# A linear-attention and MLP block on one core: the attention matrix is split one pair of chunks later, the first residual rows are asked for later, and two blocks of the matrix are copied with their column sets apart

## The chip, the cores and the metric

The kernel runs on one core of one Trainium2 chip. The metric is the device time of one launch in microseconds (us). Before the change it is 403.99 us, the median of 3 runs (402.62 to 404.39). TensorE is called PE, its weight loads PEld; VectorE is DVE, ScalarE is ACT, GpSimd is POOL and SyncE is SP. Each engine works through its own instructions in order; ACT, DVE and PE read and write on-chip tiles, SP and POOL issue the transfers (DMAs) used here, and POOL also does a little arithmetic.

## The reference

x is normalised over its 512 features, and the normalised xn goes into two branches that are added to x. All is float32.

```python
B, S, D, F, H = 1, 2048, 512, 1376, 32
xn = (x - mean(x)) / sqrt(var(x) + 1e-5)
# attention, heads of 16 features
q, k, v = split(xn @ wqkv)
phi = lambda t: where(t > 0, t + 1, exp(t)) + 1e-6
kv  = einsum("bhsd,bhse->bhde", phi(k), v)
z   = einsum("bhsd->bhd", phi(k))
o   = einsum("bhqd,bhde->bhqe", phi(q), kv) / (einsum("bhqd,bhd->bhq", phi(q), z) + 1e-6)
A   = o.reshape(B, S, D) @ wo
# MLP
h   = relu(xn @ w1 + b1) ** 2
out = x + A + (h @ w2 + b2)
```

## The kernel before

Each float32 operand of a large product is held as two parts, a high one (name ending in h, or index 0) and a low one (l, or index 1), whose sum is the number. ACT writes the high part as a copy with rounding, DVE subtracts it from the source to give the low part, and PE adds three products (high by high, high by low, low by high) in one PSUM bank. The helper `split` does the two steps; the copy is recorded at line 121 and the subtraction at line 129 or 132.

The program has four stages. First x is normalised, turned and multiplied by the key weights, and the 512 by 512 sums over tokens are gathered (lines 384 and 404). From them comes the attention matrix: kv of each head times its rows of wo, 512 by 512, in four row chunks j = 0 to 3 (`matrix`, `matrix_copy`). `matrix_copy` leaves chunk j in a raw tile `m`, two chunks to a tile, in the pool places x0 and x1; `matrix_parts(j)` then splits chunk j into `mh` and `ml` (the tiles `m[0]` and `m[1]`, 128 by 4 by 512: partition, chunk, output column).

The **first pair** are the last two blocks of 512 tokens (t1 = 3, t2 = 2). A loop `for p in range(NO + 1)` with NO = 7 goes over pairs of 128-wide chunks of the query and MLP weights (order q, w, q, w, w, w, w), two chunks by two blocks of tokens at a time. It uses seven products in place of eight (Strassen and Winograd), so each pair needs sums of weight blocks (`aop`, split into high and low) and sums of token blocks (`T[1]` to `T[4]`). In each p the four banks b0 to b3 take the products; ACT copies one (`c12`) out of its bank before PE adds to that bank again. In between `mlp_2` multiplies the squared activations of an earlier chunk by its rows of w2 into the banks `acc`. A table AT sets how many steps of the attention division (phi, weighted sum, quotient, split) go into each gap. After the loop `add_attention` multiplies the attention rows by `mh` and `ml` into `acc` for t1, and DVE adds each `acc` to the residual rows `res` (line 1096), which are then stored. `load_res(t)` asks SP for the four residual tiles of a block as two transfers of 512 KB into x0 and x1; `add_bias` has POOL add b2 onto them by four accumulating transfers of 256 KB (line 1088). Then the MLP of t2 goes on: nine `mlp_2`, numbered e = 0 to 8 below, of twelve matmuls each, their w2 parts made by ACT and DVE just ahead; attention of t2; and the last two chunks (`sum_2`). The `w2t` tiles hold sums of w2 blocks that are made there for the second pair (`w2_sums`, loads at line 1113, subtractions at 1118, stores to `w2sd` at 1121); they lie in the places B0, B1 and A0, from which the first pair's T tiles have gone and into which the second pair's T tiles are to come.

The **second pair** (t1 = 1, t2 = 0) does the chunk pairs again with operands that were stored, and then also the second product by the seven-product scheme, over output columns LO (0 to 255) and HI (256 to 511) and over pairs of rows. `mul` (line 1694) does one of the seven, M1 to M7; its part "q" is the attention's share, with the attention matrix as the stationary operand (PE loads 128 by 128 of it, then streams 512 tokens). There an output block of 256 columns is wanted as its even and its odd columns, e = 0 and 1. For operands that are sums (`mt`) they lie apart already; for the three plain blocks of `m` the helper `columns` picks every second column as PE loads the weights. M1 uses rows 0 and 1, columns LO (b11); M2 uses rows 2 and 3, columns LO (b21); M3 uses rows 2 and 3, columns HI (b22) as the moving operand, without `columns`.

Of the kernel before, what the change touches and what calls it, by code (L numbers as in the profile page):

```python
# [13 lines left out]
P = 128  # L14
# [4 lines left out]
def kernel(  # L19
# [30 lines left out]
    nc = tc.nc  # L50
# [30 lines left out]
    def bank(name, tag="ps"):  # L81
        return psum.tile([P, 512], F32, name=name, tag=tag)
# [11 lines left out]
    def two(name):  # L94
        return work.tile([P, 2, 512], F32, name=name, tag=next_tag("x"))
# [7 lines left out]
    def four(name, tag, dt=F32, pool=None):  # L103
        return (pool or work).tile([P, TB, 512], dt, name=name, tag=tag)
# [5 lines left out]
    def f32(ap):  # L110
        return ap.bitcast(F32)
# [7 lines left out]
    def copy(eng, o, i, bias=0.0):  # L119
        if eng == "act":  # L120
            nc.scalar.activation(o, i, AF.Copy, bias=bias)  # L121
        elif bias:
            ENG[eng].tensor_scalar(o, i, bias, None, op0=OP.add)
        else:
            ENG[eng].tensor_copy(o, i)
# [18 lines left out]
    def both(name, tags, dt=F32R, pool=keep):  # L144
        return [pool.tile([P, NJ, D], dt, name=f"{name}{u}", tag=t) for u, t in zip("hl", tags)]
# [262 lines left out]
    q = {}  # L408
# [151 lines left out]
    t, rk = two("x0"), four("rk", "r0")  # L560
# [7 lines left out]
    t = two("x2")  # L568
# [17 lines left out]
    for i0 in range(0, NT, TB):  # L586
        a = first_xp[i0]
# [5 lines left out]
        if i0 < NPE:  # L593
            single = work.tile([P, 3, 512], F32, name=f"xg{i0}s", tag="r0")
            for k in range(3):
                i = i0 + k - 1
# [3 lines left out]
        for k in range(0, n, 2):  # L600
            i = i0 + TB - n + k
            u, v = (t.rearrange("p a (g c) -> p (a g c)", g=NJ) for t in (a[:, TB - n + k:][:, :2], o[:, k:k + 2]))
            groups[i + 1] = [t.rearrange("p (g n) -> p g n", g=NJ) for t in (u, v)]
            u, v = (t.rearrange("p (g i c) -> p g i c", g=NJ, i=2) for t in (u, v))
# [24 lines left out]
    for k in range(2):  # L629
        a = slice(k * D // 2, (k + 1) * D // 2)  # L630
# [125 lines left out]
    def load_1(kind, n):  # L756
        load = raw_1 if kind == "w" else raw_q
        return [load(2 * n + k).rearrange("p (c n) -> p c n", c=2) for k in range(2)]
# [69 lines left out]
    def columns_low(x, t):  # L828

        for a in range(0, NJ, 2):  # L830
            rest_of(x[1][:, a:a + 2], t[:, a:a + 2], x[0][:, a:a + 2])
# [13 lines left out]
    for i in range(2, NT):  # L845
# [13 lines left out]
        ps = pks[i] if i < 3 else bank(f"pk{i}")  # L859
# [28 lines left out]
        if i == 12:  # L888
            w = load_1("q", 0)
# [67 lines left out]
    m = both("m", ("mh", "ml"), pool=work)  # L957
# [37 lines left out]
    def matrix_parts(j):  # L995
        split(m[0][:, j, :], m[1][:, j, :], mraw[j // 2][:, j % 2], "act", "dve")
# [6 lines left out]
    LO, HI = slice(0, D // 2), slice(D // 2, D)  # L1003
# [34 lines left out]
    NO = len(order)  # L1038
# [12 lines left out]
    def load_operand(p, name):  # L1051

        if p >= NO:
            return
        s, c = OPERANDS[name]
        if p % 2 == 0 and name != "A22":
            o = raw_at(f"{name}_{p}", (P, 2, 256), F32R)
        else:
            k = 7 if p % 2 == 0 else ALL_OPS.index(name)
            o = slots[k // 4][:, k % 4]  # L1060
        nc.sync.dma_start(f32(o), aopd[p][s][:, :, c * 256 % aopd[p][s].shape[-1]:][:, :, :256])
        held_ops[p][name] = [o[:, u] for u in range(2)]
# [6 lines left out]
    def second_loads():  # L1069
        slots.update({k: keep.tile([P, 4, 2, 256], F32R, name=f"slot{k}", tag=f"xT{NB // 2 + k}") for k in range(2)})  # L1070
        load_operand(0, "A22")
        for name in ALL_OPS:
            load_operand(1, name)

    def load_res(t):
        for k in range(2):
            r = two(f"res{t}_{k}")
            i = t * TB + 2 * k
            nc.sync.dma_start(r, xf[i * P:(i + 2) * P, :].rearrange("(i p) d -> p i d", i=2))
            for i in range(2):  # L1080
                res[t, 2 * k + i] = r[:, i, :]
            biased.append(r)
# [27 lines left out]
    def w2_sums(k, n, tag):  # L1110

        t = keep.tile([P, 2, 2, 512], F32, name=f"w2t{k}", tag=tag)[:, :n]
        nc.sync.dma_start(t.rearrange("p k c d -> p (k c) d"),
                          w2[2 * k * P:2 * (k + n) * P, :].rearrange("(a p) d -> p a d", p=P))
        (b11, b12), (b21, b22) = ([t[:, :, c, a] for a in (slice(0, D // 2), slice(D // 2, D))] for c in range(2))

        def less(o, x, y):
            return lambda: nc.vector.tensor_tensor(out=o, in0=x, in1=y, op=OP.subtract)

        return [less(b11, b12, b11), less(b12, b22, b12), less(b22, b22, b11), less(b21, b21, b22),  # L1120
                lambda: nc.sync.dma_start(w2sd[:, k:k + n], t)]
# [46 lines left out]
    w = load_1(*order[1])  # L1168
# [20 lines left out]
    for p in range(NO + 1):  # L1189
        at_p = AT[p]  # L1190
        kind, k = order[p] if p < NO else ("", 0)
# [64 lines left out]
        if p == 1:  # L1256
            nc.vector.tensor_scalar(zc[:, 1], zc[:, 0], 1e-6, 1e-6 * H / D, op0=OP.mult, op1=OP.add)
            acc = [bank(f"acc{t1}_{k}", "acc") for k in range(TB)]
        for j in {3: (0,), 4: (1,), 5: (2, 3)}.get(p, ()):
            matrix_parts(j)  # L1260
        step(at_p[8])
        if was == "w":
# [18 lines left out]
        if p + 2 < NO:  # L1281
            w = load_1(*order[p + 2])
# [48 lines left out]
        if p == NO - 1:  # L1331
            for k, (count, tag) in enumerate(((2, "B0"), (2, "B1"), (1, "A0"))):
                w2_prepare += w2_sums(2 * k, count, tag)
        if p == NO - 2:
            load_res(t1)
        if p == NO - 1:
            bias = add_bias()

    def wait_for(f):
# [94 lines left out]
    for k in range(TB):  # L1434
        add_attention(acc, t2 * TB + k)
        if k == 0:
# [2 lines left out]
                wait_for(f)  # L1439
            columns_low(x1, f1)  # L1440
    second_loads()
    for k in range(TB):
        for j, f in enumerate(last_two):
            sum_2(acc[k], k, f, j == 1)
        add(acc[k], t2, k)
        store(t2, k)
# [149 lines left out]
    def left_now(name, *which):  # L1596
        for part in which:
# [3 lines left out]
    RIGHT = {"M4": ("T4", "t", 1, LO), "M1": ("b11", "m", 0, LO), "M2": ("b21", "m", 1, LO), "M6": ("T2", "t", 1, HI),  # L1601
             "M5": ("T1", "t", 0, LO), "M7": ("T3", "t", 0, HI), "M3": ("b22", "m", 1, HI)}
# [72 lines left out]
    def rights(name, part):  # L1675

        key, kind, r, at = RIGHT[name]
        if part == "q":
            return [[(m if kind == "m" else mt)[u][:, 2 * r + i, at] for u in range(2)] for i in range(2)]
        return [part_at[key, k] for k in ((0, 1), (2, 3), (4,))[part]]  # L1680

    def columns(w, e, half=0):
        return w[..., half * 256:(half + 1) * 256].rearrange("p (c e) -> p e c", e=2)[:, e]

    def mul(name, ps, *which, first=False):

        for part in which:
            chunks = list(zip(half_units[name, part], rights(name, part)))
            order = [(c, e, *uv) for c in range(len(chunks)) for e in range(2) for uv in PASSES]
            order.sort(key=(lambda o: o[1]) if part == "q" else (lambda o: o[3]))  # L1690
            for c, e, u, v in order:
                a, b = chunks[c]
                w = columns(b[u], e) if part == "q" and RIGHT[name][1] == "m" else b[u][:, e * P:(e + 1) * P]
                nc.tensor.matmul(ps[e], lhsT=w, rhs=a[v], start=first and c == u == v == 0, stop=False,  # L1694
                                 skip_group_check=True)
            first = False

# [138 lines left out]
    for p in range(NO):  # L1836
        kind, k = order[p]
# [72 lines left out]
    mt = w2_start["mt"]  # L1910
# [63 lines left out]
    for parts in ((0, 1), (2, "q")):  # L1974
        chunks = [(a, b) for part in parts for a, b in zip(half_units["M3", part], rights("M3", part))]
        for k in range(TB):
            for n, (a, b) in enumerate(chunks):
                three(ends[k], [v[:, k * P:(k + 1) * P] for v in a], b, False, "q" in parts and n == len(chunks) - 1)
            if "q" in parts:
                nc.vector.tensor_tensor(out=rows[:, k], in0=ends[k], in1=rows[:, k], op=OP.add)  # L1980
                i = t1 * TB + k
# [29 lines left out]
```

## Time and profile before

| | value |
|---|---|
| median of 3 runs | 403.99 us (402.62 to 404.39) |
| the profiled execution | 403.1 us |
| its span, first to last instruction | 401.0 us |
| granted PE clock in it | 0.998 |
| DVE busy | 318.2 us, 537 instructions |
| ACT busy | 259.6 us, 434 instructions |
| POOL busy | 63.1 us, 102 instructions |
| mean DMA rate | 218 GB/s |

A row of the timeline gives the start in us from the span's start, the time taken, the engine, the line, the operation, out<-in with shapes and a count; in brackets stands the idle time before it and what ended that. Several matmuls or copies are pipelined: a matmul's row shows 0.39 us, and twelve in a row take 2.72 us, so one comes every 0.227 us. A row of the windows gives a stretch and then, for each engine, its busy time and count, the granted clock, the share of the DMA engines' time and GB/s.

### The profile page before, as it was taken

How to read it: one execution, taken by the hardware profiler on the slowest of the kernel's cores; microseconds unless marked ns; L12 is line 12 of the kernel's file. 1: busy time of each engine (PE TensorE's matmuls, PEld its weight loads, DVE VectorE, ACT ScalarE, POOL GpSimd, SP SyncE). 2: the span in 40 equal slices, each digit the busy share in tenths (PEclk: the TensorE clock that was granted, in tenths of full speed). 3: DMA queues.
4: the chain of work that ended last, by engine and by line, in shares of the span. 5: the costliest groups of instructions: out<-in, count | busy, mean ns of one | idle time of the engine just before them, and what ended most of it. 6: DMA issues, size and time to landing. Idle time of an engine off the chain costs nothing.

```text
span 401.0 us, 5834 instructions
## 1 busy us (share of the span) xinstructions
PE 394.7 (98%) x1940; PEld 326.3 (81%) x1940; DVE 318.2 (79%) x537; ACT 259.6 (65%) x434; POOL 63.1 (16%) x102
## 2 busy tenths in 40 slices
PE   7999999999999999999999999999999999999996
PEld 6788888888788877888878888888888888888895
DVE  5886666498799988997599997439999896898771
ACT  5677777556887689889555863366688666475510
POOL 5444333220410000020000200010000000232300
PEclk9999999999999999999999999999999999999999
DMA  6857647821698747689696893897798698799983
GB/s 215 274 163 240 212 157 210 230 56 30 218 329 298 259 132 254 233 269 319 213 414 266 197 209 101 286 260 236 232 270 257 188 311 178 142 226 186 172 184 108
DMA packets 80093, 87.56 MB, mean 218 GB/s; under 512 B 26304, under 2 KB 61248, under 8 KB 79296
## 3 DMA queue, kind: packets, MB, share of 16 engines
q1 hardware_dynamic: 76160, 78.27, 62.7%
q0 software_dynamic: 3824, 8.92, 12.3%
q8 instruction: 15, 0.25, 0.3%
q14 instruction: 14, 0.11, 0.1%
q10 hardware_dynamic: 80, 0.00, 0.0%
HBM read 52.05 MB, written 28.84 MB: 202 GB/s over the span
## 4 chain that ended last, share of the span: by engine, by line
PE 94%; DMA 2%; DVE 1%; ACT 1%; issue 0%; SPq 0%; ACTq 0%
PE b L528 20%; PE acc L140 18%; PE pk L384 11%; PE kx L404 11%; PE a L1694 7%; PE b_c L528 5%; PE b_a L528 4%; PE end L140 2%; PE b L1694 2%; PE y L1694 2%; PE d L1694 2%; PE b_b L528 2%; PE pz L140 1%; DMA rk<-in_A_wqkv_dram 1%; PE acc L539 1%; DMA r<-in_B_w_dram 1%
## 5 line engine op out<-in xcount | busy, mean ns | idle before, releaser
L140 PE MATMUL acc<-w2r,s 128*128 128x512 f32 x240 | 57.0, 390 | 0.0
L140 PEld LDWEIGHTS acc<-w2r,s 128*128 128x128 f32 x240 | 44.9, 188 | 9.9 <-issue 0.4
L404 PE MATMUL kx<-pk,tok 128*128 128x512 f32 x192 | 46.0, 389 | 0.0
L528 PE MATMUL b<-T,aop 128*128 128x512 f32 x168 | 42.0, 391 | 0.2 <-ACT c L121 0.2
L404 PEld LDWEIGHTS kx<-pk,tok 128*128 128x128 f32 x192 | 36.0, 188 | 7.6 <-ACT pk L121 0.2
L528 PEld LDWEIGHTS b<-T,aop 128*128 128x128 f32 x168 | 31.3, 188 | 8.1 <-ACT t L121 0.8
L365 POOL TENSOR_TENSOR tok<-xp,tok 128x512 fp32r<-128x512 f32 x15 | 19.8, 1321 | 40.0 <-ACT tok L121 40.0
L1088 POOL DMA_DIRECT2D res<-in_B_b_dram x8 | 7.1, 1012 | 108.5 <-DVE S L766 60.1
L132 DVE TENSOR_TENSOR M<-h,M 128x1024 fp32r<-128x1024 f32 (+1 forms) x15 | 15.2, 1037 | 5.0 <-ACT M L121 5.0
L121 ACT ACTIVATE T<-Tf 128x512 fp32r<-128x512 f32 x16 | 9.4, 623 | 15.0 <-DVE Tf L709 14.9
L1629 POOL DMA_DIRECT2D h<-h x6 | 5.3, 926 | 85.1 <-issue 64.5
L528 PE MATMUL b<-xs0h,aop 128*128 128x512 f32 x56 | 18.5, 392 | 0.0
L121 ACT ACTIVATE M<-h 128x1024 fp32r<-128x1024 f32 (+1 forms) x15 | 13.2, 908 | 7.5 <-PE a L1694 2.8
L121 ACT ACTIVATE pk<-k 128x512 fp32r<-128x512 f32 x16 | 10.1, 630 | 8.7 <-DVE k L379 8.7
L140 PE MATMUL acc<-mh,aTsr 128*128 128x512 f32 x48 | 15.6, 390 | 0.0
L375 ACT ACTIVATE k<-pk 128x512 f32<-128x512 f32 x16 | 9.5, 593 | 8.6 <-PE pk L384 8.6
L392 DVE SCALAR_TENSOR_TENSOR pk<-k,pk 128x512 fp32r<-128x512 f32 x16 | 11.3, 709 | 4.5 <-ACT pk L121 3.4
L132 DVE TENSOR_TENSOR w2r<-r,w2r 128x512 fp32r<-128x512 f32 (+2 forms) x20 | 13.6, 682 | 0.5 <-ACT w2r L121 0.4
L242 DVE BATCH_NORM_STATS2 st<-x 128x6 f32<-128x512 f32 x16 | 10.9, 684 | 3.6 <-DMA x<-in_A_x_dram 3.5
L384 PE MATMUL pk<-wkh,xs1h 128*128 128x512 f32 x32 | 12.7, 396 | 0.4 <-ACT xs1h L332 0.4
L379 DVE SCALAR_TENSOR_TENSOR k<-pk,k 128x512 f32<-128x512 f32 x16 | 10.8, 675 | 2.6 <-ACT k L377 2.5
L121 ACT ACTIVATE w2r<-r 128x512 fp32r<-128x512 f32 x18 | 11.1, 620 | 2.6 <-DMA r<-in_B_w_dram 2.6
(398 smaller groups left out, 1062.6 us busy)
## 6 DMA issues: line engine op xcount, KB each, us to landing
r<-in_B_w_dram SPq DMA_DIRECT2D x26, 256.0 KB, 4.8
aop_0d<-aop SPq DMA_DIRECT2D x7, 512.0 KB, 4.3
aop_1d<-aop SPq DMA_DIRECT2D x7, 512.0 KB, 5.4
aop_2d<-aop SPq DMA_DIRECT2D x7, 512.0 KB, 5.9
via<-xp SPq DMA_DIRECT2D x5, 512.0 KB, 2.6
xg<-via SPq DMA_DIRECT2D x20, 128.0 KB, 2.8
xTd<-t SPq DMA_DIRECT2D x8, 256.0 KB, 4.3
x<-in_A_x_dram SPq DMA_DIRECT2D x4, 512.0 KB, 4.1
```

The costliest lines, as they stand in the source:

```text
L121: nc.scalar.activation(o, i, AF.Copy, bias=bias)
L132: nc.vector.tensor_tensor(out=l, in0=src, in1=f32(h), op=OP.subtract)
L140: nc.tensor.matmul(ps, lhsT=a[u], rhs=b[v], start=first and n == 0, stop=last and n == 2)
L242: nc.vector.bn_stats(st[:, k, :], xr[tiles[k]])
L365: ENG[el].tensor_tensor(out=l, in0=src, in1=f32(h), op=OP.subtract)
L375: nc.scalar.activation(p, ps, AF.Relu, scale=-1.0)
L379: nc.vector.scalar_tensor_tensor(p, ps, 0.0, p, op0=OP.max, op1=OP.add)
L384: nc.tensor.matmul(ps, lhsT=cols(i)[u][:, j, slot(i)], rhs=w[v][:, j, :], start=first and n == 0, stop=last and n == len(steps) - 1)
L392: nc.vector.scalar_tensor_tensor(pk[i][:, 1], p, 1e-6, f32(pk[i][:, 0]), op0=OP.add, op1=OP.subtract)
L404: nc.tensor.matmul(kxp[c], lhsT=tok[i][:, u, c * P:(c + 1) * P], rhs=pk[i][:, v], start=i == 0 and (u, v) == first, stop=i == NT - 1 and ( ...
L528: nc.tensor.matmul(ps, lhsT=a[u][:, j * P:(j + 1) * P], rhs=b[v][:, j, :], start=first and j == 0 and n == 0, stop=last and j == 1 and n == 2,
L1694: nc.tensor.matmul(ps[e], lhsT=w, rhs=a[v], start=first and c == u == v == 0, stop=False, skip_group_check=True)
```

## The change

It has three parts.

1. `matrix_parts` for chunks 0, 1 and 2 with 3 is called at p = 4, 5 and 6 in place of 3, 4 and 5.
2. `load_res(t1)` is called at p = 6, behind the loads of `w2_sums`, in place of p = 5. (It takes the tiles out of which `matrix_parts` reads.)
3. After the last `add_attention` of the first pair, which is the last to read b12 and the old place of b11, ACT copies b11 of `mh` and `ml` to rows 0 and 1, columns HI, and then b21 to rows 0 and 1, columns LO, each with its even and odd columns apart. `mul` then reads b11 and b21 there as plain 128-column blocks.

```diff
--- before.py
+++ after.py
@@ -1256,7 +1256,7 @@
         if p == 1:
             nc.vector.tensor_scalar(zc[:, 1], zc[:, 0], 1e-6, 1e-6 * H / D, op0=OP.mult, op1=OP.add)
             acc = [bank(f"acc{t1}_{k}", "acc") for k in range(TB)]
-        for j in {3: (0,), 4: (1,), 5: (2, 3)}.get(p, ()):
+        for j in {4: (0,), 5: (1,), 6: (2, 3)}.get(p, ()):
             matrix_parts(j)
         step(at_p[8])
         if was == "w":
@@ -1331,9 +1331,8 @@
         if p == NO - 1:
             for k, (count, tag) in enumerate(((2, "B0"), (2, "B1"), (1, "A0"))):
                 w2_prepare += w2_sums(2 * k, count, tag)
-        if p == NO - 2:
+        if p == NO - 1:
             load_res(t1)
-        if p == NO - 1:
             bias = add_bias()
 
     def wait_for(f):
@@ -1439,6 +1438,10 @@
                 wait_for(f)
             columns_low(x1, f1)
     second_loads()
+    for r, to in ((0, HI), (1, LO)):
+        for t in m:
+            copy("act", t[:, :2, to].rearrange("p i (e c) -> p i e c", e=2),
+                 f32(t[:, 2 * r:2 * r + 2, LO]).rearrange("p i (c e) -> p i e c", e=2))
     for k in range(TB):
         for j, f in enumerate(last_two):
             sum_2(acc[k], k, f, j == 1)
@@ -1676,7 +1679,10 @@
 
         key, kind, r, at = RIGHT[name]
         if part == "q":
-            return [[(m if kind == "m" else mt)[u][:, 2 * r + i, at] for u in range(2)] for i in range(2)]
+            t = m if kind == "m" else mt
+            if key in ("b11", "b21"):
+                r, at = 0, HI if key == "b11" else LO
+            return [[t[u][:, 2 * r + i, at] for u in range(2)] for i in range(2)]
         return [part_at[key, k] for k in ((0, 1), (2, 3), (4,))[part]]
 
     def columns(w, e, half=0):
@@ -1690,8 +1696,7 @@
             order.sort(key=(lambda o: o[1]) if part == "q" else (lambda o: o[3]))
             for c, e, u, v in order:
                 a, b = chunks[c]
-                w = columns(b[u], e) if part == "q" and RIGHT[name][1] == "m" else b[u][:, e * P:(e + 1) * P]
-                nc.tensor.matmul(ps[e], lhsT=w, rhs=a[v], start=first and c == u == v == 0, stop=False,
+                nc.tensor.matmul(ps[e], lhsT=b[u][:, e * P:(e + 1) * P], rhs=a[v], start=first and c == u == v == 0, stop=False,
                                  skip_group_check=True)
             first = False
```

On ACT, in the pair p = 3, the rows before are these. `mh<-m` is the high part of chunk 0, `aTsr<-q` an attention split, `aop<-r` the next operands, `c_3_1645<-b` is c12, which frees the bank.

```order
L423 ACTIVATE phi<-b_0_1214 128x512
L424 ACTIVATE phi<-phi 128x512
L121 ACTIVATE mh<-m_1276 128x512
L490 ACTIVATE c_3_1566<-c_3_1566 128x512
L121 ACTIVATE s_2_1622<-c_3_1566 128x512
L121 ACTIVATE aop_0_1125<-r_4_1515 128x512
L121 ACTIVATE aTsr_1208<-q_1206 128x512
L121 ACTIVATE c_3_1645<-b_1_1215 128x512
L121 ACTIVATE aop_1_1126<-r_5_1517 128x256
```

Now the row `mh<-m` is gone from there, and c12 stands one row earlier.

```order
L423 ACTIVATE phi<-b_0_1214 128x512
L424 ACTIVATE phi<-phi 128x512
L490 ACTIVATE c_3_1566<-c_3_1566 128x512
L121 ACTIVATE s_2_1620<-c_3_1566 128x512
L121 ACTIVATE aop_0_1125<-r_4_1515 128x512
L121 ACTIVATE aTsr_1208<-q_1206 128x512
L121 ACTIVATE c_3_1643<-b_1_1215 128x512
L121 ACTIVATE aop_1_1126<-r_5_1517 128x256
```

On SP, at the end of the first pair's loop, the two residual loads (`res`) stood ahead of the last stores of operands and the loads of `w2t`.

```order
L1079 DMA res_0_1939<-in_A_x_dram 128x2x512
L1079 DMA res_1_1941<-in_A_x_dram 128x2x512
L1046 DMA aop_0d<-aop_0_1125 128x1024
L1046 DMA aop_3d<-aop_1_1126 256x1x256
L1046 DMA aop_1d<-aop_0_1125 128x1024
L173 DMA r_9_1972<-in_B_w_dram 128x512
L1046 DMA aop_2d<-aop_1_1126 128x1024
L1113 DMA w2t_2063<-in_B_w_dram 128x4x512
L1113 DMA w2t_2065<-in_B_w_dram 128x4x512
L1113 DMA w2t_2067<-in_B_w_dram 128x2x512
L1365 DMA xT_2105<-xTd_93 128x2048
L1366 DMA xT_2106<-xTd_92 128x2048
```

They now stand behind the third `w2t` load and ahead of the two `xT` loads and the five loads of w2 rows (`r`).

```order
L1046 DMA aop_0d<-aop_0_1125 128x1024
L1046 DMA aop_3d<-aop_1_1126 256x1x256
L1046 DMA aop_1d<-aop_0_1125 128x1024
L173 DMA r_9_1964<-in_B_w_dram 128x512
L1046 DMA aop_2d<-aop_1_1126 128x1024
L1113 DMA w2t_2059<-in_B_w_dram 128x4x512
L1113 DMA w2t_2061<-in_B_w_dram 128x4x512
L1113 DMA w2t_2063<-in_B_w_dram 128x2x512
L1079 DMA res_0_2065<-in_A_x_dram 128x2x512
L1079 DMA res_1_2067<-in_A_x_dram 128x2x512
L1364 DMA xT_2105<-xTd_93 128x2048
L1365 DMA xT_2106<-xTd_92 128x2048
```

On ACT, between the first and the second pair, `s_2_0` is the last activation split of the first pair, `T` are high parts for the second pair, `d<-b_a` is the second pair's first copy out of a bank.

```order
L121 ACTIVATE s_2_10_2487<-r2c 128x512
L490 ACTIVATE r2c<-r2c 128x512
L121 ACTIVATE s_2_0_2492<-r2c 128x512
L121 ACTIVATE T_1018<-Tf_2109 128x512 x2
L121 ACTIVATE T_1_2239<-Tf_2109 128x512 x2
L121 ACTIVATE d_2615<-b_a 128x512
```

The four copies of the attention matrix now stand ahead of the last four T rows; each has 128 partitions by 512 elements.

```order
L121 ACTIVATE s_2_10_2487<-r2c 128x512
L490 ACTIVATE r2c<-r2c 128x512
L121 ACTIVATE s_2_0_2492<-r2c 128x512
L121 ACTIVATE mh<-mh 128x2x256
L121 ACTIVATE ml<-ml 128x2x256
L121 ACTIVATE mh<-mh 128x2x256
L121 ACTIVATE ml<-ml 128x2x256
L121 ACTIVATE T_1018<-Tf_2109 128x512 x2
L121 ACTIVATE T_1_2239<-Tf_2109 128x512 x2
L121 ACTIVATE d_2619<-b_a 128x512
```

## Prediction

> **What bounds the kernel now.** I read the page first, then PE's waits, then the two places where the change takes work off PE's path, and last the transfers that it moves.
>
> ```profile
> PE 394.7 (98%) x1940; PEld 326.3 (81%) x1940; DVE 318.2 (79%) x537; ACT 259.6 (65%) x434; POOL 63.1 (16%) x102
> ...
> PE b L528 <- ACT c L121: 0.2, 1, 0.2
> ```
>
> The first row is the page's busy time; the second is from PE's list of waits (total, times, longest), and behind the start it is the only one there. PE is busy for 98% of the span. The change removes no matmul. So it can win little: that wait, and what single matmuls take too long. It can lose more, wherever it makes PE wait anew.
>
> **Part 1, the matrix split a pair later.** The one wait lies in p = 3, where chunk 0 was split. ACT's and PE's timelines there:
>
> ```profile
> 143.33 0.62 ACT L121 ACTIVATE mh<-m 128x512 fp32r<-128x512 f32 x1
> 143.85 0.62 ACT L490 ACTIVATE c<-c 128x512 f32<-128x512 f32 x1
> ...
> 146.08 0.58 ACT L121 ACTIVATE c<-b 128x512 f32<-128x512 f32 x1
> ```
>
> ```profile
> 143.61 1.52 PE L528 MATMUL b<-T,aop 128*128 128x512 f32 x6
> ...
> 146.10 0.39 PE L528 MATMUL b<-xs1h,aop 128*128 128x512 f32 x1
> 146.71 1.65 PE L528 MATMUL b<-T,aop 128*128 128x512 f32 x6 [0.22 <-ACT c L121]
> ```
>
> PE starts a matmul every 0.227 us, so the one at 146.71 was due at 146.33 and is 0.38 late; it waits for c12, which ACT ends at 146.66. The six behind the wait take 1.65 instead of 1.52, 0.13 more. Together the wait costs 0.51 us. Without `mh<-m` ACT gains the distance from 143.33 to 143.85, 0.52 us, and c12 ends at 146.14, before 146.33. **I take −0.51.** If the row between were held by something else, it is 0. The chain does name something else:
>
> ```profile
> 142.21 2.80 DMA r<-in_B_w_dram
> ...
> 145.04 0.37 ACT aop L121
> ```
>
> ```profile
> 128.47 5.97 SPq L192 DMA_DIRECT2D r<-in_B_w_dram x2
> ...
> 142.21 6.25 SPq L192 DMA_DIRECT2D r<-in_B_w_dram x2
> ```
>
> A load that lands at 145.01 would hold `aop<-r` at 145.04. But `aop<-r` in p = 3 reads r_4, and a pair's loads are issued one pair ahead: r_4 and r_5 are the two of 128.47 (the second by 134.4), and the load of 142.21 is r_6 for the next pair. The inferred releaser is another load on the same semaphore, and ACT was simply working without a gap.
>
> At p = 4 one split replaces another, at p = 5 one replaces two, where PE does not wait. At p = 6 two are new, 2 x 0.52 us on ACT and, at DVE's 0.60 for each of such operations in a row (four take 2.48 at 210.85 below), 1.2 on DVE, ahead of the split of c21's square:
>
> ```profile
> 188.35 0.58 ACT L121 ACTIVATE c<-b 128x512 f32<-128x512 f32 x1
> ```
>
> ```profile
> 186.12 0.68 DVE L129 TENSOR_TENSOR s<-c,s 128x512 fp32r<-128x512 f32 x1
> ```
>
> ```profile
> 189.40 2.72 PE acc L140 x12
> 192.12 1.36 PE b L528 x6
> ```
>
> The low part of s, now done at 186.8, comes at about 187.9; PE wants it at 189.40. c12, now done at 188.93, comes at about 190.0; PE wants the bank at 192.12. **0**, covered by 1.5 us.
>
> **Part 3, the column sets apart.** 24 matmuls (M1 and M2, 12 each) lose the step of two in their weights:
>
> ```profile
> L1694 PEld LDWEIGHTS a<-M_q,mth x16: 187/188/188, 360.8 to 374.0; 128*128 128x128 f32 x16
> L1694 PEld LDWEIGHTS a<-M_q,mh x8: 193/196/197, 330.6 to 332.9; 128*128 128x128 f32 x8
> ```
>
> ```profile
> 329.62 4.17 PE a L1694 x18
> ...
> 336.52 9.61 PE b L1694 x42
> ...
> 374.80 9.52 PE d L1694 x42
> ```
>
> With columns apart (`mth`) a weight load takes 188 ns, with every second column (`mh`) 196. In the chain the run of 42 that holds twelve such loads takes 9.61 against 9.52 for 42 without; 18 with twelve take 4.17 against 18 x 0.227 = 4.08. So 0.09 + 0.09, **−0.18**. The Trainium skill, SBUF — State Buffer, section "Door 1: The DMA port swizzle", speaks against this part: memory is read in 16-byte lines, and a step costs nothing while two elements of each line are used, as with a step of two float32. By that rule the term is 0 and the time 0.2 higher; the 196 beside 188 does not agree with it.
>
> The price is four ACT copies, which wait for the last `add_attention`:
>
> ```profile
> 242.10 2.18 ACT L121 ACTIVATE T<-Tf 128x512 fp32r<-128x512 f32 x4
> 256.22 0.60 ACT L121 ACTIVATE d<-b_a 128x512 f32<-128x512 f32 x1 [11.94 <-PE b_a L528]
> ```
>
> ```profile
> 247.13 0.39 PE L140 MATMUL acc<-mh,aTsra 128*128 128x512 f32 x1
> ```
>
> ```profile
> L121 ACT ACTIVATE w2r<-w2p 128x512 fp32r<-128x512 f32 x3 | 2.0, 661 | 0.0
> ```
>
> `w2r<-w2p` takes columns apart in the same way, 661 ns. Four from 247.6 end at 250.3. Behind them now stand the four T rows (2.18 us), done by 252.5, and ACT is next wanted at 256.22. **0**, inside an idle stretch of 11.94 us; even copies of 1.5 us each would fit.
>
> **Part 2, the residual rows.** The two loads pass on SP behind the third `w2t` load, which waits for PE, and POOL's four b2 transfers follow:
>
> ```profile
> 193.51 0.37 SPq L1113 DMA_DIRECT2D w2t<-in_B_w_dram x1
> ```
>
> ```profile
> res<-in_A_x_dram SPq DMA_DIRECT2D x1, 512.0 KB, 3.6
> ```
>
> ```profile
> 176.21 1.83 POOL L1088 DMA_DIRECT2D res<-in_B_b_dram x2 [60.13 <-DVE S L766]
> ...
> 180.96 0.87 POOL L1088 DMA_DIRECT2D res<-in_B_b_dram x1 [1.80 <-issue]
> ```
>
> ```profile
> res<-in_B_b_dram POOLq DMA_DIRECT2D x1, 256.0 KB, 9.4
> ```
>
> ```profile
> 190.40:199.00 8.60, 8.60 (x39) 7.10 (x38) 4.66 (x8) 4.43 (x8) 0.00 (x0) 1.00 0.61 202
> 199.00:205.00 6.00, 6.00 (x28) 4.95 (x27) 4.48 (x7) 5.82 (x11) 0.00 (x0) 1.00 0.94 383
> ...
> 227.00:235.30 8.30, 8.30 (x39) 6.86 (x38) 7.86 (x14) 6.70 (x11) 2.40 (x3) 1.00 0.97 133
> ```
>
> The loads go out at 193.9 and 194.3, when the DMA engines are busy for 0.61 of the time; with 3.6 us and the load ahead of them I put the first at 198 and POOL's first b2 transfer at 198.7. Before, the fourth was issued at 180.96 and took 9.4, so it landed 14.2 us after the first was issued; in the stretch 227.0 to 235.3, where almost only such transfers run (133 GB/s), 1.05 MB take 7.9 us, and some 1.4 to begin. So the fourth lands at 208 to 212.9. I take 212.9, because from 199 on the engines are full (0.94). Who waits:
>
> ```profile
> 210.85 2.48 DVE L1096 TENSOR_TENSOR res<-acc,res 128x512 f32<-128x512 f32 x4
> ...
> 228.72 0.68 DVE L132 TENSOR_TENSOR w2r<-r,w2r 128x512 fp32r<-128x512 f32 x1
> ```
>
> ```profile
> 209.16 39.06 PE acc L140 x171
> ```
>
> DVE wants the second residual tile for its third sum, at 210.85 + 2 x 0.60 = 212.05, so it is 0.9 us late, and it has little room to catch up (busy 7.86 of 8.30 us in the last stretch above). Its tightest product is the w2 part that ends at 229.40. PE does twelve matmuls for t1 and then twelve (2.72 us) for each chunk, so chunk e = 7 begins at 209.16 + 8 x 2.72 = 230.92 and wants that part at 231.1: a **cover of 1.7 us**. The b2 transfers also hold up what queues beside them:
>
> ```profile
> L1121 SPq DMA_DIRECT2D w2sd<-w2t x3: 320/326/327, 204.6 to 211.0; - x3
> ...
> DMA to landing us min/median/max: 3.5/4.0/6.2
> ```
>
> ```profile
> 215.17 0.64 ACT L121 ACTIVATE T<-Tf 128x512 fp32r<-128x512 f32 x1 [9.22 <-DVE Tf L709]
> ```
>
> The first store of `w2t` (204.6 + 6.2 = 210.8) must have left its place before ACT writes T there at 215.17. Held up by some 6 us of b2 traffic it leaves at about 217; ACT is then 2 us late, and DVE, which takes ACT's high parts, by my estimate 1.9: 0.2 more than the cover. **I take +0.2**; the ends are 0 (the fourth lands by 212.05) and +3.5 (the slower rival below).
>
> **Sum:** −0.51 − 0.18 + 0.2 = −0.5. The profiled execution took 403.1 (span 401.0 and 2.1 around it), so 402.6; the median of the runs shown lies 0.9 above that execution, which gives **403.5**.
>
> **Rivals.** (a) **The b2 sums come somewhat late**, at 214 to 216.5: PE waits 0.3 to 2.7 us at e = 7, 403.6 to 406.0. For it: the full engines from 199 on. Against: 14.2 us was also measured beside other traffic.
> (b) **They come much too late, and the kernel is slower.** If each 2 KB piece waits for an 8 KB packet:
>
> ```profile
> DMA packets 223, 1.70 MB, mean 424 GB/s; under 512 B 16, under 2 KB 16, under 8 KB 16
> ```
>
> In the stretch 200 to 204 a packet has 7.6 KB. 512 pieces (7.9 us) beside 512 such packets (3.9 MB at 424 GB/s, 9.2 us) take 17.1 us: the fourth lands at 198.7 + 1.4 + 17.1 = 217.2, DVE is 5.2 late, PE 3.5: net +2.8, 406.8. It decides from a landing at 213.8 on, and is measurable (0.5%, 2 us, is about what a measurement of this kernel can tell from no change) from about 216.4. Against: behind the `xT` loads (2.1 MB) come rows of 2 KB, with which the same sum gives 214. The Trainium skill, DMA: Bandwidth & Descriptors, section "Queues, rings and completion order", says that an engine takes turns between its queues packet by packet, which is this mechanism; no run here shows the order on one engine.
> (c) **The stall of p = 3 stays**, as the chain's DMA has it: 0.51 is not won, 404.0.
>
> **How the numbers follow.** Forecast 0.64 (403.5), (a) 0.17, (b) 0.08, (c) 0.09, and 0.02 for a larger gain that no row shows. Range 402.0 (the lowest run, 402.62, less the gain) to 405.8 (nearly all of (a)). Faster by over 0.5%: 0.02; within: 0.64 + 0.17 + 0.09 = 0.90; slower: 0.08.
>
> **What would show it.** PE's wait for c12 in p = 3 gone, and the six behind it at 1.52; weight loads `mh` of M1 and M2 at 188 ns; four ACT copies in 247 to 251 and no wait of PE behind them; POOL's b2 transfers beginning at 198 to 199, DVE waiting about 1 us at its third sum, PE waiting at most some tenths near 231. A first b2 transfer after 200, or a wait of PE over 2 us at 231, would make the prediction wrong.

## The result, and the profile after

| | before | after |
|---|---|---|
| median | 402.97 us (402.10 to 404.39, 6 runs) | 407.34 us (406.85 to 408.05, 6 runs) |
| the profiled execution, its span | 403.10, 401.0 us | 406.85, 404.8 us |

The ratio is 1.0105, with a 95% interval from 1.0083 to 1.0127: the changed kernel is 1% slower, 3.8 us above the forecast of 403.5 and outside its range. The outcome is that of rival (b), to which the prediction gave 0.08; its 406.8 is 0.5 from the median. One execution of sums_behind below took 810 us; its range and ratio leave it out.

From the page of after, the busy time, and from PE's list of waits (total, times, longest) the three that stand behind the start:

```profile
PE 396.6 (98%) x1940; PEld 327.0 (81%) x1940; DVE 318.6 (79%) x537; ACT 261.8 (65%) x438; POOL 63.3 (16%) x102
...
PE acc L140 <- DVE s L129: 1.7, 1, 1.7
...
PE acc L140 <- ACT w2r L121: 0.7, 1, 0.7
...
PE acc L140 <- DVE w2r L132: 0.3, 1, 0.3
```

PE's share still reads 98%. The three waits, all in the `mlp_2` products behind the first pair, are what is new. PE's timeline of after has them in place:

```profile
219.25 13.96 PE L140 MATMUL acc<-w2r,s 128*128 128x512 f32 x58 [1.66 <-DVE s L129]
233.91 0.49 PE L140 MATMUL acc<-w2r,s 128*128 128x512 f32 x1 [0.71 <-ACT w2r L121]
234.72 5.54 PE L140 MATMUL acc<-w2r,s 128*128 128x512 f32 x23 [0.32 <-DVE w2r L132]
```

Measured between the starts of matmuls, and against the pace of 0.227 us, the gaps from 219.25 to 235.06 cost 3.96 us. That is more than the 2.7 of the three brackets, since after each wait one or two further matmuls come late, and one more gap of 0.27 lies at 224.86.

The whole difference in three stretches, from the starts of PE's first product with kv (line 968) and of the first matmul after the first pair's loop (line 546): 0.18 us more ahead of the first (100.95 and 101.13), 0.67 less between the two (107.46 and 106.80), 4.26 more from the second to the end (192.63 and 196.89). That makes the 3.8 us of the spans.

The chain of waits of after leads straight to the origin (start, duration, what):

```profile
193.49 4.86 DMA res<-in_A_x_dram
...
201.81 7.18 issue
209.00 8.82 DMA res<-in_B_b_dram
...
217.91 0.13 DVE res L1096
218.03 0.48 issue
218.51 1.28 DVE s L129 x2
```

The first residual load lands at 198.35, as predicted (198). Then the four b2 transfers take until 217.81, and DVE's fourth sum stands behind them. POOL's and DVE's timelines of after:

```profile
199.09 2.73 POOL L1088 DMA_DIRECT2D res<-in_B_b_dram  x3 [82.82 <-DMA res<-in_A_x_dram]
209.00 0.87 POOL L1088 DMA_DIRECT2D res<-in_B_b_dram  x1 [7.18 <-issue]
```

```profile
211.20 1.28 DVE L1096 TENSOR_TENSOR res<-acc,res 128x512 f32<-128x512 f32 x2
213.33 0.69 DVE L1096 TENSOR_TENSOR res<-acc,res 128x512 f32<-128x512 f32 x1 [0.85 <-DMA res<-in_B_b_dram]
217.91 0.69 DVE L1096 TENSOR_TENSOR res<-acc,res 128x512 f32<-128x512 f32 x1 [3.88 <-DMA res<-in_B_b_dram]
```

The fourth sum started at 212.65 before, so DVE is 5.26 us late. From the issue of the first b2 transfer to the landing of the fourth it now takes 18.7 us, 14.2 before. Two things show how. First, the queues: of the DMA view of after, the rows of the two queues (packets, MB, share of the 16 engines) in the stretch 199 to 204, and then in 204 to 208. q0 carries POOL's transfers, q1 those of SP:

```profile
DMA packets 178, 1.35 MB, mean 270 GB/s; under 512 B 12, under 2 KB 12, under 8 KB 14
...
q1 hardware_dynamic: 178, 1.35, 88.9%
```

```profile
q1 hardware_dynamic: 191, 0.88, 57.3%
q0 software_dynamic: 176, 0.34, 48.3%
```

In the 5 us after the first issue not one packet of q0 runs (before, the first came 1.6 us after it); q1 moves the rows of `xT`, 7.6 KB a packet (1.35 MB in 178). Then the queues run 176 to 191, about one for one, though a packet of q1 still has 4.6 KB and one of q0 2. Second, three of the transfers are issued at once, and the fourth at 209.00, 0.31 us after the first has landed (208.69). Before it was the same: issued at 180.96, the first landed at 180.65.

There is a second delay of the same size. The first store of a `w2t` tile was late too. Its row in the list of line 1121 of after, and ACT's first T row:

```profile
DMA to landing us min/median/max: 12.7/13.2/15.4
```

```profile
220.44 0.63 ACT L121 ACTIVATE T<-Tf 128x512 fp32r<-128x512 f32 x1 [14.12 <-DVE Tf L709]
```

The three stores took 3.5 to 6.2 us before. The first now lands at 220.33, against 210.8, and T, which is written to its place, starts 0.11 later: 5.27 us later than before. The bracket names DVE, which had been done long ago; the wait ends with the store. So DVE and ACT are each 5.3 us late, side by side.

The smaller steps: PE and ACT in p = 3 of after, with c12 (`c<-b`) and the six that waited for it; ACT at the four copies; and M1's and M2's matmuls (line 1699 of after):

```profile
145.68 0.57 ACT L121 ACTIVATE c<-b 128x512 f32<-128x512 f32 x1
```

```profile
146.52 1.54 PE L528 MATMUL b<-T,aop 128*128 128x512 f32 x6
```

```profile
249.86 0.67 ACT L121 ACTIVATE mh<-mh 128x512 fp32r<-128x512 f32 x1 [2.41 <-PE acc L140]
...
259.88 0.60 ACT L121 ACTIVATE d<-b_a 128x512 f32<-128x512 f32 x1 [5.56 <-PE b_a L528]
```

```profile
L1699 PEld LDWEIGHTS a<-M_q,mh x8: 187/188/188, 334.3 to 336.6; 128*128 128x128 f32 x8
L1699 PE MATMUL a<-M_q,mh x8: 394/396/399, 334.5 to 336.8; 128*128 128x512 f32 x8
```

```profile
333.29 4.17 PE a L1699 x18
...
340.21 9.61 PE b L1699 x42
```

The wait of p = 3 is gone. The copies lie in an idle stretch that is still 5.56 us long behind them, and no wait of PE follows. The weight loads of `mh` fell from 196 to 188 ns as predicted, yet the runs of 18 and 42 take 4.17 and 9.61 us as before: the matmuls themselves, 396 ns each against 389 elsewhere, did not get shorter.

### The profile page after: what moved, and what is told of

Same layout as the page of the kernel before. It is cut to its first block, busy times and chain, and to the rows that moved or that the text cites. A ratio compares the mean times of both kernels' runs of the same rounds, so it can differ in the third digit from the quotient of the medians.

```text
span 404.8 us, 5834 instructions
## 1 busy us (share of the span) xinstructions
PE 396.6 (98%) x1940; PEld 327.0 (81%) x1940; DVE 318.6 (79%) x537; ACT 261.8 (65%) x438; POOL 63.3 (16%) x102
## 4 chain that ended last, share of the span: by engine, by line
PE 87%; DMA 4%; issue 3%; DVE 3%; ACT 1%; POOL 1%; SPq 0%; POOLq 0%; DVEq 0%
PE b L528 22%; PE pk L384 11%; PE kx L404 11%; PE acc L140 10%; PE a L1699 7%; PE b_c L528 5%; PE b_a L528 4%; PE end L140 2%; PE b L1699 2%; PE y L1699 2%; PE d L1699 2%; PE b_b L528 2%; DMA res<-in_B_b_dram 2%; PE pz L140 1%; DMA res<-in_A_x_dram 1%
## 5 line engine op out<-in xcount | busy, mean ns | idle before, releaser
L140 PE MATMUL acc<-w2r,s 128*128 128x512 f32 x240 | 58.2, 393 | 2.8 <-DVE s L129 1.7
```

The costliest lines, as they stand in the source:

```text
L140: nc.tensor.matmul(ps, lhsT=a[u], rhs=b[v], start=first and n == 0, stop=last and n == 2)
```

## The experiments

Each difference is against the kernel after unless it says otherwise; a time stands beside the ratio to before on the same chip, with its 95% interval.

### Which part costs the time

**loads_late**: the kernel before with part 2 alone.

```diff
-        if p == NO - 2:
-            load_res(t1)
         if p == NO - 1:
+            load_res(t1)
             bias = add_bias()
```

> The kernel before with the second part alone: the two residual loads of the first pair are asked for at p = 6, behind the w2t loads; the matrix split stays at p = 3, 4, 5 and the copies and the even-odd weight loads stay as they were. Theory L (the late residual loads push POOL's four b2 transfers into the stretch from 199 us on, where they land some 18 us after the first is issued in place of 14, and DVE's third and fourth residual sums wait for them): slower than before by 4.5 us (the change's 4.4 without the 0.7 that the gone stall of p = 3 brings, and less than 0.6 of run-to-run shift): 407.5 us, DVE waits 3 to 4 us at its fourth sum near 213.5, PE 1 to 2 us near 219. Theory S (the split at p = 6 or the copies between the pairs make PE late): within 0.5 us of before, 403 us.

Measured: 407.25 us (404.49 to 409.22), ratio 1.0112 (1.0071 to 1.0152). DVE's sums:

```profile
213.79 0.69 DVE L1096 TENSOR_TENSOR res<-acc,res 128x512 f32<-128x512 f32 x1 [2.23 <-DMA res<-in_B_b_dram]
217.70 0.69 DVE L1096 TENSOR_TENSOR res<-acc,res 128x512 f32<-128x512 f32 x1 [3.22 <-DMA res<-in_B_b_dram]
```

**split_and_copies**: parts 1 and 3 without part 2. Since the early residual loads take the tile of chunks 2 and 3, the split of p = 6 has to stay at p = 5.

```diff
-        for j in {4: (0,), 5: (1,), 6: (2, 3)}.get(p, ()):
+        for j in {4: (0,), 5: (1, 2, 3)}.get(p, ()):
...
+        if p == NO - 2:
+            load_res(t1)
         if p == NO - 1:
-            load_res(t1)
             bias = add_bias()
```

> The first and third part without the second: chunk 0 is split at p = 4 and chunks 1, 2, 3 at p = 5, the residual loads are asked for at p = 5 as before, the four copies and the plain weight blocks stay. Theory L: faster than before by 0.5 us (the stall of p = 3, 0.38 and the slow matmuls behind it), 402.4 us, no wait of PE behind the start; the b2 transfers start near 176 and end near 190. Theory S: slower than before by 2 to 4 us, 405 to 407 us, since the copies (and one split) are still there.

Measured: 402.31 us (402.07 to 403.24), ratio 0.9995 (0.9984 to 1.0005), no wait of PE behind the start. So part 2 alone makes the whole loss, and parts 1 and 3 together gain nothing that can be measured.

### Whether it is the b2 transfers

**no_b2**: the four b2 transfers of the first block are left out, so its output rows lack b2.

```diff
-            do(bias, 2)
+            bias.clear()
             mlp_2(acc, pa, s.pop(pa))
```

> The changed kernel without POOL's four b2 transfers for block 3 (its rows lack b2; block 2 and the second pair have it). Theory L, with the b2 transfers as what is late: 402.4 us, DVE's four residual sums at 211 to 214 without a wait, no wait of PE at 219 or 233. If the two residual loads themselves were what is late (they land at 198.35 and 199.65, DVE wants them at 211): as the changed kernel, 407 us. Theory S: 407 us too.

Measured: 402.26 us (401.92 to 402.67), ratio 0.9990 (0.9980 to 1.0000). DVE's sums run without a wait, ACT's T is back near its old time, and the `w2t` stores land in half the time:

```profile
211.41 2.48 DVE L1096 TENSOR_TENSOR res<-acc,res 128x512 f32<-128x512 f32 x4
```

```profile
215.72 0.63 ACT L121 ACTIVATE T<-Tf 128x512 fp32r<-128x512 f32 x1 [9.21 <-DVE Tf L709]
```

```profile
DMA to landing us min/median/max: 5.8/6.6/8.0
```

So the residual loads' later place costs nothing by itself. The 1 MB of accumulating transfers at that place costs both DVE's delay and the stores'.

**xt_pieces**: the two `xT` loads ahead of the b2 transfers go out as four loads each, with rows of 2 KB in place of 8.

```diff
-    nc.sync.dma_start(f1, xTd[t1 - 2])
-    nc.sync.dma_start(f2, xTd[t2 - 2])
+    for t, d in ((f1, xTd[t1 - 2]), (f2, xTd[t2 - 2])):
+        for j in range(NJ):
+            nc.sync.dma_start(t[:, j], d[:, j])
```

> The changed kernel with its two 1 MB loads of xT, which go out right behind the residual loads in rows of 8 KB, cut into four loads each with rows of 2 KB; the same bytes. Theory T (the DMA engines take turns between the two queues packet by packet, so beside 8 KB packets the 2 KB pieces of the b2 transfers get a small share): the first b2 transfer lands at 205 in place of 208.7, the fourth at 214 to 215 in place of 217.8, DVE waits 3 us less, 404 to 405 us. Theory B (the engines are full and each byte or each transfer has its time, whatever the packets' size): the first lands at 208 to 209, the fourth at 217 to 218, 407 us.

Measured: 405.19 us (404.51 to 407.31), ratio 1.0059 (1.0033 to 1.0085).

```profile
210.76 1.88 DVE L1096 TENSOR_TENSOR res<-acc,res 128x512 f32<-128x512 f32 x3
214.85 0.69 DVE L1096 TENSOR_TENSOR res<-acc,res 128x512 f32<-128x512 f32 x1 [2.22 <-DMA res<-in_B_b_dram]
```

The fourth lands at 214.76, 3.1 us earlier, and the loss falls by about 2 us. Of the 3.1, 0.7 is an earlier first issue (198.41); from there to the fourth's landing it takes 16.4 us in place of 18.7. So the form of the loads beside them is a real part of the delay. It need not be the packets' size alone, since the eight issues also delay the loads of w2 rows behind them on SP (first issued at 200.85, after at 197.98). The first b2 transfer lands only at 207.17 (208.69 after), later than theory T's 205, and the first packet of q0 still comes 4.4 us behind the issue. So the late beginning is not an effect of the 8 KB rows alone.

**more_scratch**: POOL's transfers get more scratch room.

```diff
-    nc = _bacc.Bacc("TRN2", target_bir_lowering=False, num_devices=1, dynamic_dma_scratch_size=1024)
+    nc = _bacc.Bacc("TRN2", target_bir_lowering=False, num_devices=1, dynamic_dma_scratch_size=1408)
```

> The kernel after, with 1408 in place of 1024 bytes of scratch room for the transfers that POOL issues; nothing else. In the kernel after the fourth b2 transfer is issued at 209.00, 0.3 us behind the landing of the first, and three are under way before. Theory R (the room holds three transfers, and the fourth waits for the first one's place): with more room the fourth is issued right behind the third, at 202 to 203. Then either its late issue was what made it late, and it lands at 213 to 215 with a time of 403.5 to 405; or the transfers were slow in any case, because their packets take turns with the others', and it lands at 216 to 218 with the third not earlier than before, and 406.5 to 407.5. Theory N (something other than the room orders them): the fourth is still issued 0.3 us behind the first one's landing, and the time is that of the kernel after, 407.3.

Measured: 404.84 us (403.87 to 406.55), ratio 1.0059 (1.0039 to 1.0079). POOL, DVE and ACT:

```profile
198.73 3.60 POOL L1088 DMA_DIRECT2D res<-in_B_b_dram  x4 [83.06 <-DMA res<-in_A_x_dram]
```

```profile
214.90 0.69 DVE L1096 TENSOR_TENSOR res<-acc,res 128x512 f32<-128x512 f32 x1 [1.62 <-DMA res<-in_B_b_dram]
```

```profile
218.66 0.63 ACT L121 ACTIVATE T<-Tf 128x512 fp32r<-128x512 f32 x1 [12.95 <-DMA w2sd<-w2t]
```

All four are now issued in a row, and the fourth lands at 214.81 in place of 217.81, 16.1 us after the first issue in place of 18.7. So the room had held back the fourth, and that was worth about half of the loss, 2 of 4 us. The first still lands at 207.90 (208.69 after) and the third at 212.37 (213.11). PE's wait for DVE's s of 1.7 us is gone; 0.7 us for ACT's and twice 0.3 for DVE's w2 parts remain.

**loads_first**: the residual loads move ahead of the `w2t` loads, which is still behind the stores of operands; POOL can start once the tile of the first load is free.

```diff
         if p == NO - 1:
+            load_res(t1)
             for k, (count, tag) in enumerate(((2, "B0"), (2, "B1"), (1, "A0"))):
                 w2_prepare += w2_sums(2 * k, count, tag)
-        if p == NO - 1:
-            load_res(t1)
             bias = add_bias()
```

> The changed kernel with the two residual loads ahead of the three w2t loads on SP, in the same p = 6: they then wait for DVE's last split there (near 187 us) and no longer for PE's last product of p = 6 (193.5). Theory T (what makes the b2 transfers late is that they run beside the 8 KB rows from 198 us on): they start near 192, the fourth lands at 205 to 208, DVE does not wait for it, no wait of PE behind the start, 402.3 us, within 0.3 of the kernel with chunks 1 to 3 split at p = 5. If the place of the split at p = 6 costs something by itself: over 403 us with PE waiting in the first pair.

Measured: 402.31 us (402.11 to 403.46), ratio 0.9994 (0.9985 to 1.0002). POOL's and DVE's rows, and one of PE:

```profile
186.31 1.83 POOL L1088 DMA_DIRECT2D res<-in_B_b_dram  x2 [70.11 <-DVE ml L129]
193.55 1.77 POOL L1088 DMA_DIRECT2D res<-in_B_b_dram  x2 [5.41 <-DVE dt L474]
```

```profile
211.88 2.48 DVE L1096 TENSOR_TENSOR res<-acc,res 128x512 f32<-128x512 f32 x4
```

```profile
146.95 1.66 PE L528 MATMUL b<-T,aop 128*128 128x512 f32 x6 [0.34 <-ACT c L121]
```

The transfers began 6 us earlier than expected. The fourth lands at 202.56, some 10 us ahead of its use, and all of the loss is gone. The split and the copies stand there unchanged. The third fence is a surprise that is taken up below: the wait of p = 3 is back, without `mh<-m` in p = 3.

### Which of the two delays PE feels

**sums_behind** takes DVE's wait away: the third and fourth residual sum of the first pair, and their stores, move behind to e = 2.

```diff
-        add(acc[k], t1, k)
-        store(t1, k)
+        if k < 2:
+            add(acc[k], t1, k)
+            store(t1, k)
...
-    acc = acc_2
+    acc_1, acc = acc, acc_2
...
         if e == 2:
+            for k in (2, 3):
+                add(acc_1[k], t1, k)
+                store(t1, k)
             load_res(t2)
```

> The changed kernel with the third and fourth residual sum and their stores moved behind the work of chunk e = 2 on DVE; the late b2 transfers stay. Theory V (DVE works in order, so the splits behind the waiting sums are late, and PE waits for those splits and not for the sums): the fourth b2 transfer still lands at 216 to 218, DVE does not wait, PE neither, 402.3 us. If the crowded transfers delay PE by another way (w2 rows or the stores of w2t that land late): PE still waits 1 to 2 us between 219 and 235, 404 to 406 us.

Measured: 406.87 us (405.07 to 407.28), ratio 1.0095 (1.0076 to 1.0115). Theory V's 402.3 did not come: nothing is won. The rows below are from a second run of the same kernel, **sums_behind_look**:

> One more look at the kernel with only the residual sums moved. Theory W: DVE does not wait at its residual sums, but ACT waits from 206 to 220 at its first T for the store of w2t that lands at 220; PE waits 1 to 2 us at 219 to 225; about 407 us.

Measured: 406.94 us (one execution), span 404.9. ACT's first T, and PE's waits:

```profile
219.57 0.63 ACT L121 ACTIVATE T<-Tf 128x512 fp32r<-128x512 f32 x1 [13.76 <-DMA w2sd<-w2t]
```

```profile
PE acc L140 <- DVE w2r L132: 2.2, 4, 1.3
...
PE acc L140 <- ACT w2r L121: 0.7, 1, 0.7
```

DVE no longer waits at its sums. Here the bracket names the store itself, and the delay reaches PE by another way: ACT stands at T, and the high parts of s and w2 behind T come late, and DVE's low parts after them.

**prep_behind** takes ACT's wait away instead: the first T of the second pair is made at e = 3 in place of e = 0, and DVE's sums stay.

```diff
-        do(prepare, (1, 0, 0, 1, 0, 2, 2, 3, 1, 3, 1)[e])
+        do(prepare, (0, 0, 0, 2, 0, 2, 2, 3, 1, 3, 1)[e])
```

> The changed kernel with the first token sum of the second pair (Tf, and ACT's T over the place of the first w2t tile) moved from e = 0 to e = 3; the residual sums stay where they wait. Theory W (two waits stand side by side, DVE's for the b2 transfers and ACT's for the first store of w2t to leave its place, each 5 us and each enough by itself): DVE still waits 4 to 5 us, 406 to 407.5 us. If ACT's wait alone is what costs: 402.3 us.

Measured: 408.34 us (407.86 to 408.62), ratio 1.0140 (1.0122 to 1.0157). DVE's fourth sum, and PE's busy time and granted clock in two stretches (the columns are those of the windows before):

```profile
217.59 0.69 DVE L1096 TENSOR_TENSOR res<-acc,res 128x512 f32<-128x512 f32 x1 [3.88 <-DMA res<-in_B_b_dram]
```

```profile
230.00:234.00 4.00, 2.70 (x12) 1.87 (x10) 3.83 (x8) 3.80 (x7) 2.40 (x3) 1.00 0.98 133
234.00:239.00 5.00, 4.70 (x14) 3.52 (x14) 4.67 (x8) 4.79 (x8) 0.86 (x1) 0.66 1.08 147
```

DVE waits for b2 as in the kernel after, and PE pays again. In this execution it pays more: from 234 to 239, right after a wait of PE, the mean granted clock is 0.66, and the 23 matmuls from 234.52 take 7.14 us where after needed 5.54, 1.6 us more. Whether that explains the 1 us between the medians is open, since five of the six executions of after have the same mean clock over the span (0.995 or 0.996).

**both_behind** has the edits of both.

> Both moves together: the third and fourth residual sum behind e = 2 and the first T behind e = 3, with the late b2 transfers left as they are. Theory W: nothing waits for the crowded transfers any more, 402.3 to 402.8 us, no wait of PE behind the start over 0.3 us. If the crowded transfers reach PE by a third way (w2 rows): over 404 us.

Measured: 402.55 us (402.24 to 403.65), ratio 0.9996 (0.9983 to 1.0008), with no wait of PE behind the start. DVE's late sums and the stores' landing:

```profile
220.48 1.28 DVE L1096 TENSOR_TENSOR res<-acc,res 128x512 f32<-128x512 f32 x2
```

```profile
DMA to landing us min/median/max: 12.3/12.8/15.0
```

The transfers are as late as in the kernel after (the fourth b2 lands at 217.77, the first store at 220.00), but nothing that PE needs stands behind them. So there were two delays side by side, each enough by itself to cost about all of the time, and neither shows its price when it alone is removed.

The three versions without the loss (split_and_copies, loads_first, both_behind) have ratios of 0.9994 to 0.9996, with intervals that hold 1: none is measurably faster than before.

### Why M1 and M2 did not get faster

**m_in_keep**: split_and_copies, with the `m` tiles in another pool, so at other addresses. The theory was that the addresses set the longer matmuls.

```diff
-    m = both("m", ("mh", "ml"), pool=work)
+    m = both("m", ("mh", "ml"))
```

> The kernel with chunks 1 to 3 split at p = 5, early residual loads and copies, with the two tiles of the attention matrix taken from the pool of the other operands, so that they and everything behind them lie at other addresses. Theory A (the pace of the 24 matmuls of M1 and M2, 0.233 us where 0.227 is usual, comes from where the tile lies, since it stayed when the step of two was gone): their pace becomes 0.227 and the runs of 18 and 42 take 4.08 and 9.52 in place of 4.17 and 9.61. Theory N (it comes from something else in these products): they keep 4.17 and 9.61. The time, 402 us, cannot tell the two apart.

Measured: 402.88 us (402.47 to 404.22), ratio 1.0006 (0.9996 to 1.0017). The runs of 18 and 42 take 4.16 and 9.60 us: the addresses are not it, as far as one other place can tell.

## Why the prediction was wrong, point by point

**What bounds the kernel** was right, and so was its conclusion: little to win, more to lose where PE waits anew.

**Part 2 is the step that failed.** The start was right: b2 from 198.7 (199.09). The term that was mis-sized is "So the fourth lands at 208 to 212.9. I take 212.9": it landed at 217.81. The upper end was 14.2 us, the time of the same four transfers in the profile of before, taken as a constant and as a bound; but it was measured beside packets of 2 to 3 KB (0.53 MB of q1 in 175 packets from 176.2 to 177.6, 2.34 MB in 1044 from 180 to 190). In the kernel after it is 18.7: some 5 us until the first packet, then turns of about one for one, at first beside packets of 4.6 KB, and then a fourth transfer that could only be issued when the first had landed. That third share was in a quoted row, 1.80 us of idle time ended by "issue" on POOL, and was not asked about. xt_pieces (18.7 us down to 16.4) and more_scratch (to 16.1) each take off a part. What it did to PE, "I take +0.2" in the sum, measured 3.96. A smaller misreading cost nothing: the third sum does not wait for the fourth transfer but for the third (it starts at 213.33, behind the landing at 213.11), so by the prediction's own 212.9 DVE would have been 0.3 late and not 0.9.

Rival (b) named the packets' turns and came to 217.2, within 0.6, with PE 3.5 late (3.96 measured). Its sum had the size right but not the whole mechanism: it has no room limit, its first packet comes after 1.4 us, where the trace shows 5, and it puts 7.6 KB beside every piece. That it came so near is in part luck. The reason against it was that rows of 2 KB come behind the `xT` loads and give 214. They do come (in 208 to 212 q1's packets have 1.8 KB, 0.50 MB in 271), and the fourth was still late, for the first 5 us were lost and it was issued only at 209.00. The Trainium skill, DMA: Bandwidth & Descriptors, section "Queues, rings and completion order", has the turns packet by packet. 176 packets beside 191 in 204 to 208 agree with it as a count; none beside 178 in 199 to 204 is not explained by it. In that section of the Trainium skill a packet typically holds 9 to 17 descriptors, while one of the profile here is mostly a single row of 2 or 8 KB; that the two are the same thing is not shown.

**The stores of `w2t`** were said to leave "at about 217", with ACT 2 us late: they left at 220.33, ACT 5.27 late. The step was on the right path, and the +0.2 of the sum came from it; what was mis-sized is "some 6 us of b2 traffic". The first store left 9.5 us later than before (220.33 against 210.81), and without the b2 transfers only 2.4 later (213.19 in no_b2). This path alone suffices to cost about all of the loss (sums_behind).

**The cover** was right in kind. It took 1.7 us at chunk e = 7 as the tightest. PE first waited at e = 2, 10.59 us behind the start of the products, for the low part of s: 1.82 us by the starts of matmuls, so the cover there was 5.26 − 1.82 = 3.4. At e = 7 what was left came out a second time, 1.56 us at 233.91 to 235.06. The 1.7 fits that: the products had begun 0.43 us earlier than before (208.66 and 209.09), and PE had by then lost 2.40, so 5.27 + 0.43 − 2.40 − 1.7 = 1.6. The two signs that the prediction named for being wrong did not come: the first b2 transfer began before 200, and no single wait was over 2 us. The loss was spread over several waits, the first of them at 219 and not near 231.

**Part 1**: "I take −0.51". Between the two marks PE took 0.67 less, and the wait is gone in the kernel after; but the reason given was only half of it. It said that ACT "was simply working without a gap". That holds from 140.54 on; the row ahead of it, which the prediction did not follow, is a wait for a load of w2 rows. ACT's row in loads_first, where that load came 0.65 us later than in after (140.66):

```profile
141.31 0.63 ACT L121 ACTIVATE w2r<-r 128x512 fp32r<-128x512 f32 x1 [3.13 <-DMA r<-in_B_w_dram]
```

There PE waits 0.34 for c12 without `mh<-m` in the way; and in loads_late, with `mh<-m` in p = 3, it does not wait at all (that load let ACT begin at 139.85). So the split's 0.52 us on ACT count only in executions in which the load is late, and the −0.51 was read from one execution; in how many of before the load is late is not known. split_and_copies shows no measurable gain on the median, but its interval (0.9984 to 1.0005) does not rule out 0.5 us either. Rival (c), a transfer upstream of ACT, was in part right, though by another load than the one that the chain named. The splits at p = 6 cost 0, as predicted.

**Part 3**: the term of −0.18 is 0. The weight loads did fall by 8 ns each, but they run beside the matmuls, and the runs of 18 and 42 kept their length. The rise to 9.61 had been put down to the step of two because the two stood together in the same rows. By the rule of the Trainium skill, SBUF — State Buffer, section "Door 1: The DMA port swizzle", the term was 0; the time agrees with it, the 196 ns of a single load did not. Why matmuls with weights from `mh` take 396 ns and those from `mth` 389 stays open. The four copies cost 0, as predicted.

## What to carry to other kernels

The time of a transfer in one place of a program is no bound for it in another: before moving one, ask what its packets will take turns with, how many of its kind the queue holds at once, and when its first packet will run. An idle row that ends with "issue" on a DMA-issuing engine can be such a limit, as it was here, and wants a question. When one late source holds up two engines, test with both waits taken away as well as each alone: here each alone showed no gain, and both together gave back all of the loss.

## What the runs showed of the hardware that was not expected

- With 1024 bytes of scratch room POOL had three transfers of 256 KB under way, and issued the fourth 0.3 us after the first landed, in before, after and xt_pieces alike; with 1408 all four went out in 3.60 us.
- POOL's transfers, issued right behind two loads of 1 MB on SP's queue, ran no packet for 5 us. In before, behind smaller loads, the first came after 1.6 us, in loads_first after 2.6. What holds them is open: rows of 2 KB in place of 8 left 4.4 us.
- After PE had waited, the mean granted clock was 0.66 in one stretch of 5 us (prep_behind), and 0.995 over the span. In five of the six executions of after the mean is 0.995 or 0.996 and the span 405.0 to 406.0, in the profiled one 1.000 and 404.8. So the 0.5 us by which the median lies above the profiled execution may be clock that the waits cost later; that was not tried by itself.
- The time of a weight load and that of its matmul were separate here: 8 ns less on the one (196 to 188) changed nothing in the other (396 before and after).
